# Windowed attention with a SoLU layer behind it: the one list that orders all five engines is laid out anew

## The chip, the cores and the metric

The kernel runs on one core of one Trainium2 chip. The metric is the device time of one launch in microseconds (us); lower is better. Its times before were 540.47 us in the median of three runs (538.63 to 542.15).

## The reference

Eight batches of eight heads with 576 positions and 64 channels go through attention with a window of 32. Heads 0 to 3 see the 32 latest positions, heads 4 to 7 every fourth of the 128 latest. The 4608 tokens of 512 values that come out go through a layer with two matrices, w_in (512 x 1024) and w_out (1024 x 512), both given in float64.

```python
scores = scale * np.matmul(q, k.transpose(0, 1, 3, 2))
scores = np.where(masks[None, :, :, :], scores, -1000000000.0)
attn = np.exp(scores - np.max(scores, axis=-1, keepdims=True))
attn = attn / (np.sum(attn, axis=-1, keepdims=True) + 1e-09)
x = np.matmul(attn, v)      # then heads side by side: (4608, 512)
h = x @ w_in
solu = h * softmax(h)
ln = (solu - mean(solu)) / np.sqrt(var(solu) + 1e-06) * g_ln
out = ln @ w_out
```

## The kernel before, in words

No scheduler decides anything here. `ORDER` (L61 to L125) is a list of 1200 words, such as `S10`, `V7` or `Ma3`: a name and a number. The kernel's last loop takes them one by one and calls the function that the table `do` has for the name; each engine gets its instructions in the order in which the words call for them. So the list sets the order on PE, DVE, ACT, POOL and in SP's queue of transfers at once. Semaphores are set where data or buffers demand it.

```python
for step in ORDER.split():
    name = step.rstrip("0123456789")
    do[name](int(step[len(name) :] or 0))
```

The words that the prediction speaks of:

- `c` loads constants, `q` and `v` load queries with keys, and values, of a unit (two heads of a batch; 32 units). `w` loads a group of weight blocks; `z` is a POOL memset that holds such a load back.
- `abs`, `low`, `hi`, `lo`, `gain` (ACT), `clamp`, `sign`, `join` (DVE) and `diff` (PE) turn the float64 weights of nine groups into a high and a low part. `ta` to `td`, `ua` to `ud`, `va` to `vd` make sums of blocks for the quick products.
- `S` n is the score word of a unit: 40 little products 32 x 64 in `scores` (L369, products at L382), which the trace shows as 80 instructions MATMUL (2560 over 32 units) and as many LDWEIGHTS. Units 0 to 5 have four more for the mask.
- `V` n is the value word, in `attend` (L466, L476): 48 or 40 little products, 96 or 80 MATMUL in the trace.
- Units go through the softmax in pairs u, as units 2u and 2u + 1: `pmask`, `pmax`, `psub`, `pexp`, `psum`, `pinv`, `pnorm`, `pturn` (DVE, but `pexp` on ACT, and `psub` and `pnorm` on POOL from pair 3 on). `pturn` (L458) is the transposition on DVE that the pair's two `V` wait for. `px` then copies the pair's results out of PSUM (ACT).
- The first matrix: for token tiles 0 to 3 the words `Ha` to `Hd` and `Ka` to `Kd`, of 3 products 128 x 512 each; from tile 4 on pairs p of tiles with the seven words `Ma` to `Mg` (a Strassen-like scheme), of 6 products each (L524). `hA`, `hB`, `hS`, `lA`, `lB`, `lS`, `s` make their operands; `ca` to `cg` take up the results.
- `peak`, `e`, `gate`, `mid`, `var`, `t`, `th`, `tl` are the SoLU and normalisation of a tile; `oa` to `od` its product with w_out, 6 products 128 x 512 each (L696); `out` stores it.

A product 128 x 512 is one LDWEIGHTS and one MATMUL. "Large products" below are those of `H`, `K`, `M`, `o` and `diff`; "small words" are `S` and `V`.

Of the kernel before, what the change touches and what calls it, by code (L numbers as in the profile page):

```python
# [58 lines left out]
LOWS = "t0 t1 e0 e1 w12 w13 x_sum w12".split()  # L59
H_BANK = {0: 2, 1: 0, 2: 2, 3: 0}  # L60
ORDER = (  # L61
# [63 lines left out]
)  # L125
PRODUCTS = {
    "Ma": (0, (0, 2), 0), "Mb": (8, (16, 17), 1), "Mc": (2, (4, 6), 0), "Md": (10, (21, 19), 1),
# [715 lines left out]
```

## Time and profile before

| | us |
|---|---|
| three runs: median (lowest to highest) | 540.47 (538.63 to 542.15) |
| the profiled execution: its time | 538.95 |
| its span, from the first to the last instruction | 536.4 |
| PE busy | 482.4 (90%) |
| DVE, ACT, POOL busy | 403.1 (75%), 315.9 (59%), 172.0 (32%) |

The span is what the rows of the trace add up to; 538.95 - 536.4 = 2.55 us lie around it. Times in the rows count from the span's start. A matmul's end is modelled, so that its successors seem to begin before it ends: a stream is timed from start to start. "Idle before" names what ended an engine's idle time; "issue" means that the engine waited for nothing that the profile shows.

### The profile page before, as it was taken

Reading aid. Unit: us, or ns where it says so; the run is one execution under the profiler, and the core shown is the slowest. Engines: PE = TensorE matmul, PEld = TensorE weight load, DVE = VectorE, ACT = ScalarE, POOL = GpSimd, SP = SyncE. Lnnn points to the kernel's source line nnn. Section 1 sums busy time; section 2 is a strip of 40 time slices with the busy share of each in tenths; the row PEclk is TensorE's granted clock in tenths of the full one; section 3 lists DMA queues with packets and bytes.
Section 4 is the critical chain, followed back from the end, with each engine's and each line's share of the span. In section 5 each row is a group of like instructions: output and inputs, shape, how many; then the busy total and the mean of one; then the engine's idle time right before and its main releaser. Section 6 shows DMA issues by size and latency. Waiting matters only on the chain.

```text
span 536.4 us, 16190 instructions
## 1 busy us (share of the span) xinstructions
PE 482.4 (90%) x7116; PEld 385.5 (72%) x7116; DVE 403.1 (75%) x632; ACT 315.9 (59%) x415; POOL 172.0 (32%) x262
## 2 busy tenths in 40 slices
PE   4648869899979799999998989998999899999997
PEld 2235658777858677788777767886887688888885
DVE  1887978898786598877778867797898967786341
ACT  3757778756545266664545655765483736466571
POOL 0202446632415053333423306242505243131121
PEclk9978979999979799999998989999999999999999
DMA  8991520321935423534441434443725141231011
GB/s 308 377 377 66 185 79 1 129 69 40 304 108 153 145 86 114 143 83 146 137 137 50 119 126 129 129 133 130 222 81 147 29 123 43 77 99 40 21 39 39
DMA packets 32693, 66.57 MB, mean 124 GB/s; under 512 B 3568, under 2 KB 18160, under 8 KB 32240
## 3 DMA queue, kind: packets, MB, share of 16 engines
q1 hardware_dynamic: 32480, 65.42, 38.2%
q8 instruction: 55, 0.90, 0.7%
q10 hardware_dynamic: 144, 0.13, 0.1%
q14 instruction: 14, 0.11, 0.1%
HBM read 41.42 MB, written 9.44 MB: 95 GB/s over the span
## 4 chain that ended last, share of the span: by engine, by line
PE 53%; DVE 23%; issue 8%; ACT 6%; POOL 5%; DMA 3%; SPq 1%; DVEq 0%; ACTq 0%; POOLq 0%
PE banks L696 24%; PE banks L524 18%; PE banks L476 6%; PE banks L382 3%; DVE t L614 3%; DVE x_lo L328 2%; POOL sm L455 2%; DVE pt L458 2%; DMA u<-b 2%; POOL sm L434 1%; DVE little L420 1%; DVE tl L328 1%; DVE little L445 1%; DVE sm L404 1%; DMA wt<-w_in 1%
## 5 line engine op out<-in xcount | busy, mean ns | idle before, releaser
L696 PE MATMUL banks<-wt,th 128*128 128x512 f32 x576 | 181.0, 398 | 1.3 <-ACT ob L713 1.2
L696 PEld LDWEIGHTS banks<-wt,th 128*128 128x128 f32 x576 | 107.7, 190 | 25.9 <-ACT ob L713 2.6
L696 PE MATMUL banks<-wt,tl 128*128 128x512 f32 x288 | 112.2, 393 | 0.0
L524 PE MATMUL banks<-wt,x_hi 128*128 128x512 f32 x320 | 103.2, 404 | 1.6 <-ACT wt L333 1.1
L524 PEld LDWEIGHTS banks<-wt,x_hi 128*128 128x128 f32 x320 | 60.7, 193 | 15.3 <-ACT wt L333 1.7
L524 PE MATMUL banks<-w,x_hi 128*128 128x512 f32 x192 | 63.2, 411 | 1.2 <-DVE t L578 1.2
L524 PE MATMUL banks<-wt,x_lo 128*128 128x512 f32 x160 | 63.9, 399 | 0.3 <-DVE x_lo L328 0.3
L434 POOL TENSOR_TENSOR sm<-sm,little 128x1280 f32<-128x1280 f32 x13 | 32.6, 2505 | 96.7 <-DVE little L420 78.0
L696 PEld LDWEIGHTS banks<-wt,tl 128*128 128x128 f32 x288 | 54.7, 190 | 11.7
L585 DVE CUSTOM_DVE_ANT_0 t<-banks,t 128x512 f32<-128x512 f32 x64 | 43.3, 685 | 24.1 <-PE banks L524 23.4
L608 ACT ACTIVATE e<-t,row 128x1024 f32<-128x1024 f32 x32 | 36.8, 1150 | 30.4 <-DVE row L591 30.4
L476 PE MATMUL banks<-pt,vt 32*64 32x64 f32 (+3 forms) x2816 | 35.9, 238 | 20.4 <-issue 15.2
L713 ACT ACTIVATE ob<-banks,row 128x512 f32<-128x512 f32 x35 | 24.0, 686 | 50.3 <-PE banks L696 36.2
L476 PEld LDWEIGHTS banks<-pt,vt 32*64 32x64 f32 x2816 | 33.6, 139 | 26.9 <-issue 18.1
L614 DVE CUSTOM_DVE_ANT_0 t<-t,e 128x1024 f32<-128x1024 f32 x32 | 40.5, 1269 | 9.6 <-ACT e L608 9.6
L382 PE MATMUL banks<-qk 64*32 64x64 f32 x2560 | 33.1, 235 | 14.9 <-issue 12.5
L669 ACT CAST th<-u 128x1024 fp32r<-128x1024 f32 x28 | 29.3, 1047 | 27.4 <-DMA u<-b 22.7
L382 PEld LDWEIGHTS banks<-qk 64*32 64x32 f32 x2560 | 28.4, 110 | 23.6 <-issue 17.5
L524 PEld LDWEIGHTS banks<-w,x_hi 128*128 128x128 f32 x192 | 36.6, 196 | 10.6 <-DVE t L578 2.2
L639 POOL TENSOR_SCALAR row<-row 128x1 f32<-128x1 f32 x36 | 8.8, 245 | 103.9 <-ACT e L634 102.8
L492 ACT COPY x_raw<-banks 128x1152 f32<-128x1152 f32 x16 | 26.9, 1682 | 23.3 <-PE banks L476 23.1
L635 POOL TENSOR_SCALAR row<-row 128x1 f32<-128x1 f32 x36 | 20.0, 555 | 64.3 <-ACT e L608 62.2
(107 smaller groups left out, 819.0 us busy)
## 6 DMA issues: line engine op xcount, KB each, us to landing
qk<-qk SPq DMA_DIRECT2D x32, 616.0 KB, 5.4
u<-b SPq DMA_DIRECT2D x112, 128.0 KB, 2.9
vt<-vw SPq DMA_DIRECT2D x32, 384.0 KB, 4.6
out<-ob SPq DMA_DIRECT2D x35, 256.0 KB, 2.4
wt<-w_out SPq DMA_DIRECT2D x4, 1024.0 KB, 10.8
wt<-w_in SPq DMA_DIRECT2D x3, 1024.0 KB, 14.3
wt<-w_in SPq DMA_DIRECT2D x2, 512.0 KB, 8.1
steady_sb<-steady SPq DMA_DIRECT2D x1, 260.0 KB, 4.1
```

The costliest lines, as they stand in the source:

```text
L382: nc.tensor.matmul(out=ps[WIN * c : WIN * c + WIN, h, WQ * i : WQ * i + WQ], lhsT=qt[D * h : D * h + D, q0 : q0 + WIN], rhs=kt[D * h : D * ...
L434: eng.tensor_tensor(out=rows(part(sm_sb, us)), in0=soft_source(us), in1=mx, op=ALU.subtract)
L476: nc.tensor.matmul(out=ps[D * h : D * h + D, c, c0 : c0 + k1 - k0], lhsT=vt[WIN * c : WIN * c + WIN, i, D * h : D * h + D], rhs=pt[WIN * c ...
L492: nc.scalar.copy(out=x.rearrange(form, c=NG), in_=ps[:, k : k + len(us), :, 0:GQ])
L524: nc.tensor.matmul(out=ps, lhsT=a[:, x], rhs=weights(w)[:, part, :], start=start and k == 0 and j == 0, stop=stop and k == last and j == 2 ...
L585: nc.vector.tensor_tensor_reduce(out=split_t(k)[half], in0=banks[:, c, :], in1=add, scale=1.0, scalar=-3.0e38, op0=ALU.add, op1=ALU.max, a ...
L608: nc.scalar.activation(out=e_sb[i % 2], in_=h_of(i), func=AF.Exp, bias=ms[i]["nmax"], scale=1.0, accum_out=se)
L614: nc.vector.tensor_tensor_reduce(out=t_sb[i % 2], in0=h_of(i), in1=e_sb[i % 2], scale=1.0, scalar=0.0, op0=ALU.mult, op1=ALU.add, accum_ou ...
L635: nc.gpsimd.tensor_scalar(out=se, in0=se, scalar1=1e-9, scalar2=None, op0=ALU.add)
L669: nc.scalar.copy(out=by_quarter(th), in_=u_sb[i % 2].rearrange("p g (k i) -> p k g i", k=FT))
L696: nc.tensor.matmul(out=ps_o(i), lhsT=a[:, f, :], rhs=weights(8 + f)[:, part, :], start=k == 0, stop=k == 3 * FT - 1,)
L713: nc.scalar.activation(out=ob, in_=ps_o(i), func=AF.Copy, scale=rstd)
```

## The change

Only `ORDER` is changed: the same 1200 words stand in another order, and no function differs. With them go all five engines and SP's queue. In the opening the loads go `c w0 w1 w2 q1 q0 w3 w4`, where they went `q0 c w1 q1 w0 w2 w3 w4`. Behind the opening the words `S` and `V` take other places. Before, the two `S` of each of the 16 pairs stand next to each other on PE, and the two `V` also. Now large products stand between the two `S` of five pairs (1, 2, 5, 6, 15) and between the two `V` of six (3, 6, 8, 12, 13, 15); the other pairs still stand together, at other places among the products. Between the later `S` of a pair and its first `V` there were at least 11 words of six large products in pairs 4 to 15; now there are 10 in pairs 5, 6, 7 and 14, 11 in pairs 4 (with the transpositions `t2` and `t3` besides), 13 and 15, and 13 or more in the others. The lines around pair 6 and pair 5:

```diff
-    "pnorm5 od2 pturn5 Mc3 hA4 tl5 Md3 V11 cd3 V10 Mf3 cc3 q14 ce3 cf3 out2 px5 Mg3 lA4 oa5 S13 "
-    "th4 v15 tl4 S12 hB4 e7 s4 ob5 gate7 hS4 cg3 mid7 oc5 q16 pmask6 pmax6 e6 od5 t7 out5 Ma4 "
...
+    "v13 e5 s3 v11 px4 cg2 ob3 lB3 S10 gate5 oc3 od3 hS3 e4 mid5 S11 out3 gate4 lS3 mid4 pmask5 "
+    "var5 pmax5 psub5 Ma3 t5 oa2 var4 Me3 ca3 Mb3 pexp5 Mc3 t4 ob2 cb3 Md3 psum5 th5 hA4 pinv5 oc2 "
+    "od2 out2 th4 q13 cd3 Mf3 cc3 pnorm5 pturn5 lA4 q12 V10 ce3 V11 Mg3 tl4 px5 Ma4 cf3 tl5 cg3 "
+    "oa5 s4 e6 gate6 hS4 S12 lS4 ob5 e7 gate7 oc5 s5 mid7 S13 pmask6 mid6 od5 pmax6 Mb4 psub6 out5 "
```

On PE, the score words of pair 6 (units 12 and 13) before; L382 with x40 is one `S`, an L696 row with `th` and x2 and one with `tl` are three large products:

```order
L696 MATMUL banks<-wt_723,th_1028 128x512 x2
L696 MATMUL banks<-wt_723,tl_1065 128x512
L696 MATMUL banks<-wt_723,th_1028 128x512 x2
L696 MATMUL banks<-wt_723,tl_1065 128x512
L382 MATMUL banks<-qk_83 32x64 x40
L382 MATMUL banks<-qk_82 32x64 x40
L696 MATMUL banks<-wt_706,th_1028 128x512 x2
L696 MATMUL banks<-wt_706,tl_1065 128x512
```

The same two words now:

```order
L382 MATMUL banks<-qk_82 32x64 x40
L696 MATMUL banks<-wt_737,th_1020 128x512 x2
L696 MATMUL banks<-wt_737,tl_1053 128x512
L696 MATMUL banks<-wt_737,th_1020 128x512 x2
L696 MATMUL banks<-wt_737,tl_1053 128x512
L696 MATMUL banks<-wt_684,th_1020 128x512 x2
L696 MATMUL banks<-wt_684,tl_1053 128x512
L696 MATMUL banks<-wt_684,th_1020 128x512 x2
L696 MATMUL banks<-wt_684,tl_1053 128x512
L382 MATMUL banks<-qk_83 32x64 x40
```

Twelve large products have come between the two score words.

On DVE, the softmax of pair 2 in the opening before (L420 is `pmax2`, L434 `psub2`, L604 `peak0`, L445 `psum2`, L614 `gate0`, L449 and L450 `pinv2`, L455 `pnorm2`, L458 `pturn2`):

```order
L420 TENSOR_REDUCE little<-banks 128x20
L434 TENSOR_TENSOR sm<-banks,little 128x1280
L604 TENSOR_REDUCE row<-banks 128x1
L445 TENSOR_REDUCE little<-sm 128x20
L614 ISA t_71,row<-banks,e_73 128x1024
L614 ISA row 128x1
L449 TENSOR_SCALAR little<-little 128x20
L450 RECIPROCAL little<-little 128x20
L624 TENSOR_SCALAR row<-row 128x1
L455 TENSOR_TENSOR sm<-sm,little 128x1280
L458 STREAM_TRANSPOSE pt<-sm 128x1280
```

The same stretch of DVE now:

```order
L420 TENSOR_REDUCE little<-banks 128x20
L434 TENSOR_TENSOR sm<-banks,little 128x1280
L445 TENSOR_REDUCE little<-sm 128x20
L449 TENSOR_SCALAR little<-little 128x20
L450 RECIPROCAL little<-little 128x20
L455 TENSOR_TENSOR sm<-sm,little 128x1280
L458 STREAM_TRANSPOSE pt<-sm 128x1280
L604 TENSOR_REDUCE row<-banks 128x1 x2
```

`peak0` and `gate0` (with its L624) have gone behind `pturn2`.

## Rows read from the trace of the kernel before

**Rows 1.** The page: busy time, share of the span, instructions; DMA queue, kind: packets, MB

```profile
PE 482.4 (90%) x7116; PEld 385.5 (72%) x7116; DVE 403.1 (75%) x632; ACT 315.9 (59%) x415; POOL 172.0 (32%) x262
...
q8 instruction: 55, 0.90, 0.7%
```

**Rows 2.** PE's waits from 93 us on: engine line <- awaited: total us, times, longest

```profile
PE banks L476 <- issue: 10.0, 4, 3.4
PE banks L382 <- issue: 7.5, 5, 2.5
...
PE banks L476 <- DVE pt L458: 0.8, 3, 0.4
```

**Rows 3.** PE's timeline, 149 to 162 us: start, length, what, count [idle before <- releaser]

```profile
150.50 1.48 PE L382 MATMUL banks<-qk 64*32 64x64 f32 x128 [0.62 <-issue]
154.50 0.45 PE L382 MATMUL banks<-qk 64*32 64x64 f32 x12 [2.52 <-issue]
154.88 1.22 PE L696 MATMUL banks<-wt,th 128*128 128x512 f32 x2
...
160.17 0.79 PE L696 MATMUL banks<-wt,th 128*128 128x512 f32 x2
...
161.03 0.62 PE L696 MATMUL banks<-wt,th 128*128 128x512 f32 x2
...
161.71 0.62 PE L524 MATMUL banks<-wt,x_hi 128*128 128x512 f32 x2
```

**Rows 4.** PE's timeline at other "issue" waits

```profile
34.47 0.42 PE L382 MATMUL banks<-qk 64*32 64x64 f32 x3 [3.89 <-issue]
34.82 2.16 PE L476 MATMUL banks<-pt,vt 32*64 32x32 f32 x125
41.04 1.25 PE L476 MATMUL banks<-pt,vt 32*64 32x64 f32 x67 [4.06 <-issue]
...
126.16 1.40 PE L382 MATMUL banks<-qk 64*32 64x64 f32 x119 [0.21 <-issue]
...
174.04 1.96 PE L476 MATMUL banks<-pt,vt 32*64 32x32 f32 x171
179.43 0.61 PE L476 MATMUL banks<-pt,vt 32*64 32x48 f32 x21 [3.42 <-issue]
```

**Rows 5.** Windows (three of the five): us, busy us (count) of PE, PEld, DVE, ACT, POOL, PEclk, DMA share, GB/s

```profile
153.68:160.51 6.83, 6.01 (x25) 4.68 (x26) 5.44 (x4) 1.73 (x3) 2.31 (x1) 0.50 0.30 96
177.57:184.40 6.83, 4.97 (x143) 3.90 (x145) 1.08 (x5) 2.07 (x2) 0.00 (x0) 0.50 0.20 60
...
426.75:430.16 3.41, 3.41 (x10) 2.64 (x9) 2.86 (x3) 1.72 (x3) 0.97 (x4) 0.50 0.62 134
```

**Rows 6.** DVE's timeline in the opening

```profile
46.16 1.51 DVE L458 STREAM_TRANSPOSE pt<-sm 128x1280 f32<-128x1280 f32 x1
47.59 1.18 DVE L303 SCALAR_TENSOR_TENSOR tl<-tl,x_sum 128x1024 int32<-128x1024 int32 x1
...
61.13 1.22 DVE L604 TENSOR_REDUCE row<-banks 128x1 f32<-128x1024 f32 x1
...
63.96 1.22 DVE L614 CUSTOM_DVE_ANT_0 t<-banks,e 128x1024 f32<-128x1024 f32 x1
...
69.65 1.51 DVE L458 STREAM_TRANSPOSE pt<-sm 128x1280 f32<-128x1280 f32 x1
```

**Rows 7.** PE's timeline: the value words of pairs 2 and 3

```profile
71.21 2.79 PE L476 MATMUL banks<-pt,vt 32*64 32x32 f32 x188 [4.31 <-DVE pt L458]
...
93.14 1.78 PE L476 MATMUL banks<-pt,vt 32*64 32x64 f32 x148
```

**Rows 8.** PE's timeline: end of the score words of pair 13

```profile
373.29 1.63 PE L382 MATMUL banks<-qk 64*32 64x64 f32 x136
```

**Rows 9.** DVE's timeline: the transpositions of pairs 6 and 13

```profile
171.17 1.51 DVE L458 STREAM_TRANSPOSE pt<-sm 128x1280 f32<-128x1280 f32 x1 [0.99 <-POOL sm L455]
...
387.40 1.51 DVE L458 STREAM_TRANSPOSE pt<-sm 128x1280 f32<-128x1280 f32 x1
```

120 rows, old and new, of the table ORDER are left out of this document.

## The prediction, written before the changed kernel ran

> **What bounds the kernel now.** I read the page first, to see which engine is full: PE, busy for 482.4 of 536.4 us, 90% [rows 1]. So the time is PE's work plus what PE loses, and I looked for the losses: in the list of waits, then in PE's timeline around the longest of them, then in windows for the granted clock.
>
> The list of waits gives the first loss. From 93 us on, when the opening is over, PE stands idle for 10.0 + 7.5 = 17.5 us in front of small products (L476, L382) with no releaser but "issue"; the wait for the softmax (DVE pt) is 0.8 us in all [rows 2]. The timeline shows where such a wait stands. The two S words of pair 6 are 160 MATMUL in a row. PE stops before 128 of them, runs those 128 in 1.48 us, stops for 2.52 us and does the last 12 [rows 3]. The same spacing stands in the opening: a stop, 3 + 125 = 128 MATMUL, a stop [rows 4]. 128 MATMUL with their 128 LDWEIGHTS are 256 instructions. The page's queue q8 moved 0.90 MB of instructions in 55 packets, and PE has 2 x 7116 instructions: 259 for each packet of 16.4 KB [rows 1]. I read this so: PE's program comes in blocks of 256 instructions, and the next block is usable only some time after the one before it was entered. With "line" for a block's beginning, that time can be read where PE had to wait: 154.50 - 150.50 = 4.0 us behind one line; in the opening, under the weight loads, 41.04 - 34.47 = 6.6 us [rows 3, 4]. A block of nothing but small products lasts 1.5 us, so it costs a stop of 2 to 3 us. A block with some large products lasts longer and costs little: the one that ends where the 119 MATMUL at 126.16 begin has six by my count (below), and the stop behind it is 0.21 us [rows 4].
>
> The second loss hangs on the first. In the windows the granted clock is 0.50, the lower of TensorE's two levels, from 153.68 to 160.51, from 177.57 to 184.40, and in three shorter windows of 3.4 us, each of which holds or follows such a stop [rows 5]. Twelve large products take 160.17 - 154.88 = 5.29 us there, and three take 161.71 - 161.03 = 0.68 us at the full level, which is 2.72 us for twelve [rows 3].
>
> **The change part by part.** It adds and removes nothing: the products are the same, at 0.68 / 3 = 0.227 us each. The sum goes against the profiled execution's span, 536.4 us.
>
> 1) The stops behind the opening, 17.5 us. I counted PE's list in steps of 256 instructions, a large product 2, an S word 160, a V word 192 or 160, from the line that row 34.47 fixes (three MATMUL before the end of the S words of pair 1), with some forty instructions that only wait counted too. In the list of before, behind pair 2's V words, eight blocks hold no large product at all: in the V words of pairs 3, 6, 10, 12 and 13 and the S words of pairs 6, 10 and 15; long stops stand at seven of them, all but pair 13's. In the new list no block there is without: one has 6 (V6, ob0 and V7), three have 9 or 10, all others 12 or more. Twelve large ones are 12 x 0.227 = 2.7 us, and with 116 small ones at 1.48 / 128 = 0.0116 us the block lasts 4.1 us, against the 4.0 us of row 150.50. The block with 6 lasts 1.4 + 1.4 = 2.8 us and may wait 0.2 (as at 126.16) to 1.2 us. Where a fetch takes as long as in the V words of pair 6, a block of twelve waits too: there 43 of the 171 MATMUL at 174.04 still belong to the block before (0.5 us), so it was 179.43 - 174.54 = 4.9 us [rows 4], 0.8 us more than the block lasts. I keep 2.5 us: -15.0, with ends -17.5 (all gone) and -10 (most blocks meet slow fetches).
>
> 2) The half clock. The five windows are 2 x 6.83 + 3 x 3.41 = 23.9 us. Of these PE waited 154.50 - 153.68 = 0.8 and 179.43 - 177.57 = 1.9 us, and some 2.5 us went to small words, whose pace falls little; half of the 18.7 us left is lost: -9.2. Without stops of 2 us I see nothing that would lower the level. Ends -9.2 and -5.
>
> 3) The opening. DVE sets it from 47 us on: pair 1's transposition ends at 47.67, pair 2's at 71.16, and PE idles 4.31 us until then [rows 6, 7]. Of the 23.5 us between, three operations go to the other side: join7 (1.18) ahead of the first transposition, peak0 and gate0 (1.22 each) behind the second [rows 6]; two shorter ones change sides and about cancel. That leaves 19.9 us. Ahead of pair 1's transposition, join7 is added, and the waits that PE's two stops of 3.89 and 4.06 us passed on to DVE [rows 4] are largely gone: S3 and S2 have diff3 between them, which gives the fetch its time. I put pair 1 at 44, so pair 2 at 64 and its V words 7 us earlier. From there to pair 3's V words it was 93.14 - 71.21 = 21.9 us [rows 7]; peak0 and gate0 come into this stretch (2.4 us at worst), while PE's loss in the first of these V words goes, so I keep 22: V6 at 86, but with six large products fewer before it (ob0 goes behind): 93.14 - 86 - 1.36 = 5.8 us gained. Against this stands the order of the loads: S0 now waits for three weight groups that go ahead of q0. Ends +1 and -10; I take -5.8.
>
> 4) New waits. Fewer stops, and S and V nearer to each other, give the softmax less room: what a pair needs from its last S to the end of pturn. Pair 13 shows 387.40 + 1.51 - 373.29 - 1.63 = 13.99 us, pair 6 shows 171.17 + 1.51 - 154.50 - 0.45 = 17.7 us [rows 3, 8, 9], both with PE not waiting or hardly. Between S and V pairs 5, 6, 7 and 14 now have ten words of six, 10 x 1.36 = 13.6 us; pairs 13 and 15 have 15.0. I take 14.5 us, near pair 13, since the new list puts pturn right ahead of V there, and pair 6 had 12 words and two stops to fill: 4 x 0.9 = +3.5, with ends 0 (13.6) and, at 15.6, 4 x 2.0 + 2 x 0.6 = +9. Queued behind a waiting V on PE are the large products of the next M and o, whose results DVE and ACT take up, so such a wait is not made good by other work.
>
> Sum: 536.4 - 15.0 - 9.2 - 5.8 + 3.5 = 509.9 us, and with the 2.55 us around the span 512.5. The profiled execution (538.95) was 1.5 us under the median, so 512.5 to 514; I forecast 513 us.
>
> [...]
>
> **The rivals.**
>
> a) The softmax takes over in part. DVE is at 75% [rows 1] and 27 us less time makes it 79%; each pair then needs 16 us from S to pturn. Four pairs wait 2.4 us and two 1.0, 11.6 us, and four waits over 2 us bring the half clock back at 9.2 / 5 = 1.8 us each: 18.8 us in place of 3.5, 528 us. For it: pair 6's 17.7 us. Against it: pair 13, and 0.8 us of such waits in all before.
>
> b) The stops stay. Either PE's program is there in time, and the idle time before small products is one that the order doesn't move; or my count of the lines is off by some tens of instructions, and S and V pairs that still stand together cover whole blocks again. Terms 1 and 2 fall away: 536.4 - 5.8 + 3.5 + 2.55 = 537 us, within 1% of before. [...] For the second: the new places hold by some tens of instructions only. Against both: stops 128 MATMUL apart, in two places [rows 3, 4], and a count that finds seven long stops of before.
>
> c) Slower: the chain S to pturn becomes the bound. If it needs 18.7 us, one more than pair 6 took, four pairs wait 5.1, two 3.7, pair 4 (16.9 us of room, two transpositions counted) 1.8, three with 13 words (17.7 us) 1.0 each: 32.6 us, with six half-clock windows 10.9 more. 43.5 - 15.0 - 9.2 - 5.8 = +13.5: 552 us. It decides from some 17.5 us on, where waits and clock eat the 30 us gained. Against it: POOL and DVE work on other things between a pair's steps when V isn't near, so 17.7 is no floor, and 14.0 was made.
>
> **How the numbers follow.** A difference of 1% is about what a measurement of this kernel can tell from none. My forecast, from 500 to 522 us, has a chance of 0.70; a) (522 to 534) 0.17; b) 0.08; c) 0.05. Faster: forecast and nearly all of a), 0.87; within 1% (535.1 to 545.9): b), 0.08; slower 0.05. The best ends of the terms give 536.4 - 17.5 - 9.2 - 10 + 2.55 = 502; the worst of the forecast 536.4 - 10 - 5 + 1 + 9 + 2.55 = 534, but not all at once. The range goes from 502 to 529, which takes in a) and leaves out b), c) and the tails.
>
> **What would show it.** Step 1: the "issue" waits of PE behind the opening fall from 17.5 us to under 5, and none is over 1.5 us. Step 2: granted clock 1.00 in all of the span from about 90 us on. Step 3: pair 2's V words begin near 64 us, pair 3's near 86. Step 4: waits for DVE pt at the V words of pairs 5, 6, 7 and 14, about 1 us each. Wrong would be: stops at other words with the same 128 MATMUL between them (b), or V words that wait 3 us and more with DVE's L458 as releaser (a, c).

## The result, and the profile after

| | before | after |
|---|---|---|
| runs beside each other: median (lowest to highest), us | 540.32 (538.63 to 542.15), 4 runs | 511.92 (510.17 to 514.58), 4 runs |
| ratio to before, 95% interval | | 0.948 (0.943 to 0.953) |
| the profiled execution: time, span | 538.95, 536.4 | 514.58, 512.8 |
| PE busy | 482.4 (90%) | 476.2 (93%) |

The changed list is 28.4 us faster in the median; 513 us had been forecast, in a range of 502 to 529. The two profiled executions are 24.4 us apart, because the one of before lay 1.4 us under its median and the one of after 2.7 us over its own. Their spans differ by 23.6 us, and these the trace accounts for. Ratios, here and below, leave out executions more than 1.5% above the fastest of their kernel, while medians take in all of them; of the kernel before, which spreads from 530.5 to 543.0 us over 19 executions, the ratios see the faster part alone.

The page of the kernel after, its busy times, PE's load in 40 slices and the granted clock, and the instruction queue (packets, MB, share):

```profile
PE 476.2 (93%) x7116; PEld 382.3 (75%) x7116; DVE 389.2 (76%) x632; ACT 315.4 (62%) x415; POOL 156.7 (31%) x262
...
PE   1958779999999998999999999998999999999997
...
PEclk9987779999999999999999999999999999999999
...
q8 instruction: 55, 0.90, 0.7%
```

The count of instructions and the 55 packets of program are those of [rows 1]; what has changed is that PE is nearly gapless from the seventh slice on, and that the clock there stays at its higher level: its two levels in the traces of before and after are 0.50 and 1.00, and from 78.4 to 511.8 us it is 1.00.

PE's waits in the kernel after, from 93 us on, as in [rows 2] (engine line <- awaited: total us, times, longest):

```profile
PE banks L382 <- issue: 3.3, 2, 1.8
PE banks L524 <- DVE t L578: 1.0, 1, 1.0
PE banks L382 <- ACT x_raw L492: 0.9, 1, 0.9
PE banks L382 <- DMA qk<-qk: 0.8, 1, 0.8
PE banks L476 <- issue: 0.6, 2, 0.4
...
PE banks L476 <- DMA vt<-vw: 0.2, 1, 0.2
```

The 17.5 us of "issue" have become 3.3 + 0.6 = 3.9 us, and the wait for the softmax (DVE pt) isn't in the list at all.

S8, the first score word of pair 4, begins at 99.93 us before and at 98.55 after, and both lists have the same PE work behind it. So the stretch from there to the end can be compared window by window (columns as in [rows 5]). Before:

```profile
99.90:536.40 436.50, 412.90 (x5593) 336.72 (x5592) 326.39 (x548) 247.82 (x332) 138.72 (x225) 0.97 0.37 110
```

After:

```profile
98.50:512.80 414.30, 404.11 (x5592) 330.23 (x5592) 315.33 (x544) 247.95 (x331) 128.04 (x228) 1.00 0.38 115
```

The same 5592 products take 412.90 - 404.11 = 8.8 us less, because the granted clock is 1.00 and no longer 0.97: that is the half-clock loss. PE's idle time falls from 436.50 - 412.90 = 23.6 to 10.2 us, 13.4 us less; 12.0 of it are "issue" stops (15.7 us from 100 us on before, 3.7 after), 1.4 other waits. Together 22.2 us; the other 1.4 us of the 23.6 by which the spans differ come from the opening, in this pair of executions.

PE's timeline of the kernel after: all the stops that are left (start, length, what, count [idle before <- releaser]):

```profile
39.35 1.25 PE L476 MATMUL banks<-pt,vt 32*64 32x64 f32 x68 [2.89 <-issue]
...
55.04 0.65 PE L382 MATMUL banks<-qk 64*32 64x64 f32 x23 [2.78 <-issue]
...
94.41 0.32 PE L476 MATMUL banks<-pt,vt 32*64 32x16 f32 x12 [0.18 <-issue]
...
172.50 0.66 PE L476 MATMUL banks<-pt,vt 32*64 32x64 f32 x39 [0.37 <-issue]
...
200.31 1.19 PE L382 MATMUL banks<-qk 64*32 64x64 f32 x99 [1.75 <-issue]
...
351.68 0.71 PE L382 MATMUL banks<-qk 64*32 64x64 f32 x47 [1.58 <-issue]
```

The one at 94.41 stands behind the block with six large products, where 0.2 to 1.2 us had been foreseen. The two long ones, at 200.31 and 351.68, stand behind blocks of 18 and 12 large products, and data were being loaded there. The window ahead of the first of them:

```profile
192.80:197.90 5.10, 5.10 (x107) 4.07 (x101) 3.53 (x10) 5.02 (x5) 0.00 (x0) 1.00 0.72 251
```

PE worked in all of the 5.10 us, with the 16 DMA engines at 0.72, and still had to wait 1.75 us for its next block. Neither of the two was followed by the half clock.

### The profile page after: what moved, and what is told of

Its sections match the earlier page's. It is cut to its first block, busy times and chain, and to the rows that moved or that the text cites. A ratio compares the mean times of both kernels' runs of the same rounds, so it can differ in the third digit from the quotient of the medians.

```text
span 512.8 us, 16184 instructions
## 1 busy us (share of the span) xinstructions
PE 476.2 (93%) x7116; PEld 382.3 (75%) x7116; DVE 389.2 (76%) x632; ACT 315.4 (62%) x415; POOL 156.7 (31%) x262
## 4 chain that ended last, share of the span: by engine, by line
PE 71%; DMA 11%; DVE 7%; ACT 4%; SPq 3%; issue 3%; POOL 0%; ACTq 0%; DVEq 0%; POOLq 0%
PE banks L696 32%; PE banks L524 28%; PE banks L476 5%; PE banks L382 4%; DMA vt<-vw 4%; DMA wt<-w_in 3%; DMA qk<-qk 2%; SPq L658 2%; DMA u<-b 2%; ACT x_raw L492 1%; DVE t L614 1%; PE banks L651 1%; DVE tl L328 1%; DVE row L604 1%; PE banks L324 1%
## 5 line engine op out<-in xcount | busy, mean ns | idle before, releaser
L696 PE MATMUL banks<-wt,th 128*128 128x512 f32 x576 | 179.4, 395 | 0.0
L696 PEld LDWEIGHTS banks<-wt,th 128*128 128x128 f32 x576 | 106.1, 188 | 22.9 <-ACT ob L713 0.8
L696 PE MATMUL banks<-wt,tl 128*128 128x512 f32 x288 | 111.1, 390 | 0.0
L524 PE MATMUL banks<-wt,x_hi 128*128 128x512 f32 x320 | 104.2, 408 | 2.3 <-DVE row L614 1.8
L524 PEld LDWEIGHTS banks<-wt,x_hi 128*128 128x128 f32 x320 | 60.4, 194 | 16.1 <-DVE row L614 1.9
L524 PE MATMUL banks<-wt,x_lo 128*128 128x512 f32 x160 | 63.9, 399 | 0.0
L434 POOL TENSOR_TENSOR sm<-sm,little 128x1280 f32<-128x1280 f32 x13 | 31.3, 2407 | 105.3 <-DVE little L420 91.2
L696 PEld LDWEIGHTS banks<-wt,tl 128*128 128x128 f32 x288 | 54.1, 188 | 11.6
L524 PE MATMUL banks<-w,x_hi 128*128 128x512 f32 x192 | 59.9, 393 | 1.0 <-DVE t L578 1.0
L585 DVE CUSTOM_DVE_ANT_0 t<-banks,t 128x512 f32<-128x512 f32 x64 | 43.0, 682 | 12.2 <-PE banks L524 11.6
L382 PE MATMUL banks<-qk 64*32 64x64 f32 x2560 | 32.9, 237 | 16.5 <-DMA qk<-qk 8.7
L382 PEld LDWEIGHTS banks<-qk 64*32 64x32 f32 x2560 | 28.5, 110 | 25.3 <-issue 11.7
L578 DVE TENSOR_TENSOR t<-banks,t 128x512 f32<-128x512 f32 x32 | 21.9, 685 | 28.9 <-PE banks L524 23.0
L629 ACT ACTIVATE t<-t,row 128x1024 f32<-128x1024 f32 x28 | 31.9, 1149 | 17.8 <-DVE row L624 17.8
L614 DVE CUSTOM_DVE_ANT_0 t<-t,e 128x1024 f32<-128x1024 f32 x32 | 39.5, 1243 | 3.7 <-ACT e L608 3.6
L524 PEld LDWEIGHTS banks<-w,x_hi 128*128 128x128 f32 x192 | 35.5, 188 | 8.9 <-DVE t L578 1.7
L328 DVE TENSOR_TENSOR tl<-u,th 128x1024 fp32r<-128x1024 f32 x28 | 34.0, 1219 | 7.9 <-ACT th L669 7.7
```

The source lines that it names most:

```text
L328: eng.tensor_tensor(out=out, in0=whole, in1=part.bitcast(F32), op=ALU.subtract)
L382: nc.tensor.matmul(out=ps[WIN * c : WIN * c + WIN, h, WQ * i : WQ * i + WQ], lhsT=qt[D * h : D * h + D, q0 : q0 + WIN], rhs=kt[D * h : D * ...
L434: eng.tensor_tensor(out=rows(part(sm_sb, us)), in0=soft_source(us), in1=mx, op=ALU.subtract)
L524: nc.tensor.matmul(out=ps, lhsT=a[:, x], rhs=weights(w)[:, part, :], start=start and k == 0 and j == 0, stop=stop and k == last and j == 2 ...
L585: nc.vector.tensor_tensor_reduce(out=split_t(k)[half], in0=banks[:, c, :], in1=add, scale=1.0, scalar=-3.0e38, op0=ALU.add, op1=ALU.max, a ...
L614: nc.vector.tensor_tensor_reduce(out=t_sb[i % 2], in0=h_of(i), in1=e_sb[i % 2], scale=1.0, scalar=0.0, op0=ALU.mult, op1=ALU.add, accum_ou ...
```

## The experiments

The theory: PE's program arrives in blocks of 256 instructions, a block of tiny products alone is over before the next is there, and the new list puts enough large products into every block. Its rival: the places of the blocks don't matter; the gain is that other words stand next to each other, so that PE waits less for the other engines. The two differ where the list stays and only the block lines move. Ratios are to runs of the kernel before on the same chip. The kernels are set against each other by their medians.

**Moving the lines without moving the work.** A word `pad64` of 64 products of 32 columns, 128 PE instructions whose result nothing reads, goes ahead of S8 into the changed list; a second kernel has 32 of them (half as many), a third 128, a whole block:

```diff
+    def pad(n):
+        for _ in range(n):
+            nc.tensor.matmul(
+                out=banks[0:32, 4, 420:452], lhsT=id_bf[:, 0:32], rhs=id_bf[:, 0:32],
+                start=True, stop=True, skip_group_check=True,
+            )
...
-    lA2 ub1 od0 S8 vb1 out0
+    lA2 ub1 od0 pad64 S8 vb1 out0
```

64 products, half a block:

> The changed list with one word more: 64 products 32 x 32 (bf16, 128 instructions, into a part of PSUM that nobody reads) right ahead of S8. Nothing else moves. Theory (lines every 256 instructions): the lines behind that point fall 128 instructions earlier among the words, and the count finds eight blocks with no or one large product again where the changed list had none. Eight stops of 1.5 to 3 us come back, 13 to 18 us, with half-clock windows 5 to 10 us more, and about 1 us for the 64 products: 532 to 540 us. Rival (what counts is which words stand beside S and V, and what the other engines do meanwhile): only the 64 products are paid, 512.5 to 514 us.

128 products, a whole block:

> The changed list with 128 such products (256 instructions) right ahead of S8. Theory: the lines fall by a whole block, so among the words behind they stand where the changed kernel has them, and one block of nothing but these products is added: 1.5 to 2 us for them, one stop of about 2 us, perhaps one half-clock window of 2 us, 515 to 518 us, and less than with half as many products. Rival: twice the price of the 64 products, more than with 64.

32 products, a quarter of a block:

> The changed list with 32 of the little products (64 instructions) right ahead of S8; they take about 25 ns each, as in the run with 128, so 0.8 us. Theory: behind that point the count finds four blocks with no or one large product and one with four, where the changed list has none and the list with 64 products eight. Stops of 6 to 10 us come back, with one to three half-clock windows 2 to 5 us: 519 to 526 us, between the changed kernel and the one with 64 products. Rival: 0.8 us more than the changed kernel, 513 us.

| changed list with | median, us | ratio to before | PE "issue" from 100 us on | S8 to the end |
|---|---|---|---|---|
| nothing | 511.92 | 0.948 (0.943 to 0.953) | 3.7 | 414.3 |
| 32 products | 527.27 | 0.976 (0.969 to 0.983) | 12.1 | 429.4 |
| 64 products | 528.06 (10 runs) | 0.987 (0.981 to 0.993) | 14.2 | 431.5 |
| 128 products | 518.37 | 0.974 (0.969 to 0.979) | 3.3 | 414.8 |

The last two columns are of the profiled executions; that of the 64 products took 531.73 us, 3.7 over its median. Its waits of PE, from 100 us on (columns as above):

```profile
PE banks L476 <- issue: 6.3, 3, 3.4
PE banks L382 <- issue: 4.1, 4, 1.8
PE banks L524 <- issue: 3.8, 4, 1.7
PE banks L476 <- DMA vt<-vw: 1.2, 1, 1.2
PE banks L382 <- DMA qk<-qk: 1.1, 1, 1.1
```

The stops are back, though no word of the list has another neighbour, and no wait for DVE or ACT of note has come with them. They even stand before large products (L524), where the waits of neither list show one behind S8. Two of them in PE's timeline, and the window behind the second:

```profile
362.11 1.34 PE L382 MATMUL banks<-qk 64*32 64x64 f32 x111 [1.82 <-issue]
...
410.53 0.32 PE L476 MATMUL banks<-pt,vt 32*64 32x16 f32 x12 [3.44 <-issue]
```

```profile
411.20:414.60 3.40, 3.40 (x10) 2.62 (x9) 1.12 (x4) 1.51 (x3) 0.00 (x0) 0.50 0.02 5
```

Windows of this kind, at a granted clock of 0.50, stand behind four of its stops. The whole block of pads, with twice the products, is 9.7 us faster than the half: the lines are where they were, and little more than the pads is paid for (518.37 - 511.92 = 6.4 us, of which 3.3 are the pads and 1.4 a stop behind them). The rival, by which all three would cost no more than their own length, falls. Two of the three ranges were missed a little: 518.37 lies 0.4 us above its own (515 to 518), 528.06 lies 4 us under its own (532 to 540). In the list with half a block, seven blocks behind S8 hold no large product and one holds two; with a quarter, four hold none or one; in the changed list none does. The price doesn't follow that count (16.1 and 15.4 us): the quarter had been put at 519 to 526 and is beyond it. One reason is in the trace: three of the seven blocks, with lines at 143.50, 264.81 and 389.56 us, cost no stop. Their lines stand at most 16 small products behind large ones, and the packet with the next block (these packets are looked at below, at the nine S8) begins 1.0 to 2.0 us before such a line, at 141.50, 263.62 and 388.56. The changed list's layout is good for the one phase that it was counted for.

**One half of the list at a time.** Up to S8 the one list and from S8 on the other (the few words that would be missing or double are brought ahead of S8 or left out behind it).

The list of before up to S8, the changed one behind:

> The list of before up to S8, the remaining words in the changed order. Theory: the stops behind 93 us (17.5 us before) fall to about 4 and the half clock there (9 us) is gone; the opening is as before, V6 at about 93 us: 511 to 515 us, as the opening of the changed kernel gained only 1 us. Rival (the gain comes from the opening and from what it does to the rest): over 525 us.

The changed list up to S8, the one of before behind:

> The changed list up to S8, the remaining words in the order of before. Theory: stops behind 93 us as before, all seven long ones at the same words, and the half clock after them: 535 to 540 us. Rival (the opening carries the gain): under 525 us.

| | median, us | ratio | "issue" from 100 us on | S8 begins | S8 to the end |
|---|---|---|---|---|---|
| before | 538.66 (19 runs) | | 15.7 | 99.9 | 436.5 |
| new remainder | 516.7 | 0.971 (0.965 to 0.978) | 1.0 | 102.1 | 415.1 |
| new opening | 534.0 (10 runs) | 1.001 (0.997 to 1.005) | 16.2 | 98.4 | 438.3 |
| after | 511.92 | 0.948 (0.943 to 0.953) | 3.7 | 98.5 | 414.3 |

(First row: time of these 19 runs, columns of the profile before.) The remainder is worth 538.66 - 516.7 = 22.0 us, the opening 538.66 - 534.0 = 4.7 us, and in the other order 511.92 beside 534.0 and 516.7 gives 22.1 and 4.8. By its ratio of 1.001 the new opening alone is worth nothing, so that its share is not settled between none and some 5 us; the remainder's is clear by either. How early S8 begins speaks for a gain: 99.9, 102.1 and 104.3 us in three executions with the old opening, 97.3 to 98.6 us in five with the new (where pads stand ahead of S8, the first of them begins at 96.6, 96.8 and 99.5). The medians lie beside the expected ranges: 516.7 is 1.7 us above 511 to 515, 534.0 is 1 us under 535 to 540. With the old remainder the old stops stand at the old words, as in [rows 3, 4]:

```profile
151.93 1.49 PE L382 MATMUL banks<-qk 64*32 64x64 f32 x128 [0.97 <-issue]
...
155.94 0.33 PE L382 MATMUL banks<-qk 64*32 64x64 f32 x12 [2.52 <-issue]
...
179.84 0.41 PE L476 MATMUL banks<-pt,vt 32*64 32x48 f32 x21 [3.50 <-issue]
```

**One word of the list of before.** S12 goes behind oc5, so that twelve large products (ob5 and oc5) come between the score words of pair 6, whose stop of 2.52 us stands in [rows 3].

```diff
-    th4 v15 tl4 S12 hB4 e7 s4
+    th4 v15 tl4 hB4 e7 s4
...
-    cg3 mid7 oc5 q16 pmask6
+    cg3 mid7 oc5 S12 q16 pmask6
```

> The kernel before with one word moved: S12 stands behind oc5, twelve large products behind S13, where it stood next to it. Theory: the block between 150.50 and 154.50 us then holds twelve large products, its stop of 2.52 us goes and with it the half-clock window from 153.68 to 160.51 (2.6 us): 4 to 6 us less than before, if pair 6's softmax, with 10 words left to its V instead of 12, makes it in 14 us; all other stops stay. Rival (the stops belong to score and value words wherever they stand): the stop moves along, no difference.

538.02 us in the median of 10 runs (540.06 before), ratio 0.994 (0.988 to 1.000): too little to be told by the time alone. In the trace the stop and its half clock are gone, and from S10 to V14 it is 75.1 us, where it was 78.5. The expected 4 to 6 us came out as 3.4, and the rows of pair 6's value words show why:

```profile
174.28 1.97 PE L476 MATMUL banks<-pt,vt 32*64 32x32 f32 x171 [0.85 <-DVE pt L458]
180.36 0.62 PE L476 MATMUL banks<-pt,vt 32*64 32x48 f32 x21 [4.11 <-issue]
```

PE comes to V13 before the transposition is done (0.85 us), and at the next line, which hasn't moved, it stops for 4.11 us in place of 3.42 [rows 4]: the block came no sooner for PE being ahead. One stop less gave its length less what was late next.

**The price of a block by itself.** S8 stands nine times in the changed list: 8 x 160 = 1280 instructions more, five blocks of tiny products and nothing else.

```diff
-    od0 S8 vb1 out0
+    od0 S8 S8 S8 S8 S8 S8 S8 S8 S8 vb1 out0
```

> The changed list with S8 nine times in a row (the same products into the same place, 8 x 160 = 1280 instructions more, five whole blocks). It measures the disputed cost by itself: how fast PE gets through small products when its program has to be fetched for them alone. Theory: stops with 128 MATMUL between them, 3.4 to 4 us from stop to stop, five of them: 16 to 20 us more than the changed kernel (528 to 532 us), the stops behind as in the changed kernel. Rival (small products in a row are only bound by their issue): 8 x 1.0 us = 8 us more, 520 us.

One run: 536.11 us, 24 us more than the changed list, for 16 to 20 expected. PE's timeline:

```profile
98.27 2.49 PE L382 MATMUL banks<-qk 64*32 64x64 f32 x232 [1.45 <-ACT x_raw L492]
103.20 1.49 PE L382 MATMUL banks<-qk 64*32 64x64 f32 x128 [2.44 <-issue]
109.67 2.06 PE L382 MATMUL banks<-qk 64*32 64x64 f32 x128 [4.99 <-issue]
113.13 2.06 PE L382 MATMUL banks<-qk 64*32 64x64 f32 x128 [1.40 <-issue]
116.86 2.05 PE L382 MATMUL banks<-qk 64*32 64x64 f32 x128 [1.67 <-issue]
120.58 1.12 PE L382 MATMUL banks<-qk 64*32 64x64 f32 x56 [1.68 <-issue]
```

and its windows, from the second of these rows to the third and from the third to the last:

```profile
103.20:109.67 6.47, 1.49 (x128) 1.32 (x128) 0.00 (x0) 0.09 (x1) 0.00 (x0) 0.72 0.68 224
109.67:120.58 10.91, 6.16 (x384) 5.44 (x384) 0.00 (x0) 0.00 (x0) 0.00 (x0) 0.50 0.02 5
```

The stops are 128 MATMUL and 128 LDWEIGHTS apart, four times in a row, at words that wait for no other engine. With the DMA engines nearly still (0.02), from line to line it takes 113.13 - 109.67 = 3.46 us, then 3.73 and 3.72; with them at 0.68 it took 6.47. The 232 that ran without a stop are the last 104 of one block and the 128 of the next: one block was there in advance here, not several. The five stops make 12.2 us, and the 640 MATMUL at full clock 7.4; the rest of the 24 us fits the half clock, which lasts to 126.5 us and at which 128 of these products take 2.06 and not 1.49 us.

The blocks can be seen to arrive: the trace times each packet of q8, the queue of the instructions. Behind the line at 103.20 the DMA engines move data alone until 107.20, and in the 0.1 us after that the packet begins (windows 103.20 to 107.20, then 107.20 to 107.30; queue, kind: packets, MB, share of the 16 engines):

```profile
q1 hardware_dynamic: 353, 1.23, 94.9%
...
q1 hardware_dynamic: 15, 0.03, 78.4%
q8 instruction: 1, 0.02, 62.2%
```

Behind the line at 109.67, with nothing else to move, the packet begins at 110.82 (window 110.80 to 110.90):

```profile
q8 instruction: 1, 0.02, 61.8%
```

The five stops end 2.3 to 2.7 us after the beginning of a packet (at 100.85, 107.22, 110.82, 114.17 and 117.92). The same holds in all twelve traces: from 93 us on they have 65 stops of over 0.15 us that end without a releaser, and each ends 2.2 to 3.3 us after a packet's beginning. At each, too, PE's MATMULs and LDWEIGHTS so far, divided by 256, give in whole blocks the number of packets begun. So the "issue" of these stops is PE waiting for its program. What made a fetch late was the time before its packet began. Behind the lines that a stop marks it is 1.0 to 1.7 us with the DMA engines at less than 0.15, with one exception (3.0 us); in 13 cases it is 2.4 us or more, and in all of these but that one the engines were at 0.74 to 1.02 meanwhile. Two lines of the kernel before lie between, with 1.88 us at 0.55 (283.14 us) and 1.96 us at 0.99 (310.42 us).

**The changed list once more, and two attempts to better it.** The first kernel is the changed list itself; the second has S5 behind Ka0, to give the fetch ahead of the stop at 55.04 more time; the third brings four loads to places away from the two stops that were left (q17 up behind S13, as shown, q18 down behind S17, q29 and v29 down behind S26).

```diff
-    sign6 clamp6 yd0 S5 v5 Ha0 hi7 Ka0 v4
+    sign6 clamp6 yd0 v5 Ha0 hi7 Ka0 S5 v4
```

```diff
-    oc6 cb5 od6 q17 th9 q18 out6
+    oc6 cb5 od6 th9 out6
...
-    s5 mid7 S13 pmask6
+    s5 mid7 S13 q17 pmask6
```

> The changed list once more, on the chip of the three runs beside it. 509 to 515 us, as its first four runs (510.2 to 514.6).

> The changed list with S5 moved behind Ka0, so that nine large products instead of three stand between S4 and S5. Theory: the opening's gain was small because PE stops there too: the stop of 2.78 us at 55.04 falls under 1 us, V4 comes 1.5 to 2.5 us earlier than at 67.4, the whole 1 to 3 us under the changed kernel. Rival (DVE bounds the opening): V4 stays at 67 to 68, no difference.

> The changed list with four loads moved: q17 up behind S13, q18 behind S17, q29 and v29 behind S26. PE's order is the same. Theory (a block's fetch comes late while loads fill the DMA engines): the stops of 1.75 us at 200.31 and 1.58 us at 351.68 go, both of which stand behind blocks with 18 and 12 large products in which the DMA share was 0.72 and 0.88: 2 to 4 us under the changed kernel. Rival (those two are something else): they stay at the same words.

Medians of 511.97 (ratio 0.952, 0.943 to 0.960), 512.37 (0.951, 0.945 to 0.957) and 512.7 us (0.953, 0.946 to 0.960): no difference. With S5 moved PE still stops, and the window ahead of the stop shows a thing that the place of the word doesn't change:

```profile
56.68 0.45 PE L382 MATMUL banks<-qk 64*32 64x64 f32 x29 [2.45 <-issue]
```

```profile
50.00:53.50 3.50, 3.50 (x95) 2.56 (x94) 1.49 (x3) 3.50 (x6) 0.01 (x1) 1.00 0.98 379
```

The DMA engines are full (0.98) while the block is due; its packet begins at 54.24. With the loads moved, the stop near 352 us stayed (1.86 us), since SP issued the loads ahead of it when it had before (qk, vt and qk from 343.27 to 345.04 us, against 342.65 to 344.08 in the kernel after). The stop at 200.31 is gone there: SP issues one load of qk ahead of that block (at 192.30 us) where it issued two in the kernel after (from 190.37), and the packet begins 1.8 us behind the line and no longer 5.1. The same block in the other traces of this list fits: 4.3 us and a stop of 0.88 in the plain repetition, 3.4 us and no stop with S5 moved. So late fetches went with data being moved, in these four and in the windows shown here (DMA share 0.72, 0.68 and 0.98); each is one execution, and no run took the traffic away and nothing else. No kernel here beats the changed one.

## Why the prediction was right

**The reading of the bound** holds. Blocks of 256 instructions, and a new block some 4 us after the last line, or later under load: the nine S8 words show both (3.46 to 3.73, and 6.47 us), the pads show that the places of the lines decide and not the neighbours, and the packets of the instruction queue stand ahead of every stop. Why pair 13's block of before cost no stop, which the prediction left open, is to be seen there too: the packet with the next block begins at 388.57 us, 1.5 us before the line at 390.07, which stands six small products behind large ones. The nine S8 also show why a block of products of 12 ns alone is over too soon: its 128 MATMUL with their loads are through in 1.5 us, and the next block came 3.46 to 6.47 us after it was entered. Rival b) falls in both its forms: the program was not there in time, and the count of the lines was right. That a shift by some tens of instructions would undo the gain was right too, by 15 us for 64.

**Term 1, the stops behind the opening:** -15.0 forecast, 3.9 - 17.5 = -13.6 measured. The allowance of 2.5 us for late fetches was 1.4 short, and two stops are over the 1.5 us that the forecast set as the longest: it took the fetch of 4.9 us for the slow case, and at 192.80 the packet alone began 5.1 us behind the line. The count had left out one short block, the one right behind pair 2's V words (from 71.79 us, with about five large products by the trace); it cost no stop.

**Term 2, the half clock:** -9.2 forecast (half of 18.7 is 9.35, a slip of 0.15), -8.8 by PE's busy time for the same 5592 products. The forecast let the pace of the small words fall little; at 0.50 it fell more than that (128 products took 2.06 us in the nine S8, and 1.49 at full clock). In the kernel after the clock is 1.00 from 78.4 to 511.8 us. Not every stop brought the lower level: the two of 1.75 and 1.58 us in the kernel after were followed by none, while one of 1.71 us with S5 moved was (0.50 from 349.0 to 352.4 us).

**Term 3, the opening:** -5.8 forecast, measured to V6: by the same reckoning it is 93.14 - 90.73 - 1.36 = 1.05 us in the two profiled executions, and up to S8 between nothing (ratio) and 4.7 us (medians) in the half lists. This is the term that was furthest off. DVE's part came nearly as worked out. Pairs 1 and 2 in DVE's timeline after, beside [rows 6]:

```profile
41.83 1.51 DVE L458 STREAM_TRANSPOSE pt<-sm 128x1280 f32<-128x1280 f32 x1
...
63.67 1.51 DVE L458 STREAM_TRANSPOSE pt<-sm 128x1280 f32<-128x1280 f32 x1
```

They end at 43.3 and 65.2 us, for 44 and 64 forecast; the stretch between them took 21.8 us, 2 more than the 19.9 of the forecast. But PE doesn't follow:

```profile
67.35 2.19 PE L476 MATMUL banks<-pt,vt 32*64 32x32 f32 x192
71.34 1.07 PE L524 MATMUL banks<-wt,x_hi 128*128 128x512 f32 x2 [1.80 <-DVE row L614]
...
90.73 1.08 PE L476 MATMUL banks<-pt,vt 32*64 32x64 f32 x80
```

V4 begins at 67.35 without a wait: by then PE itself is late, from its stop at 55.04 and the half clock behind it (0.50 from 54.5 to 61.3 us). Behind V5 it waits 1.80 us for gate0 (L614), one of the two operations that went behind the transposition (2.4 us at worst, in the forecast), and the clock is at 0.50 again until 78.4; in the repetition of the same list the wait was the same and the clock stayed up. V6 came at 90.73 and not at 86. The step that failed is the one that let PE be ready whenever DVE was: it counted the two stops of before as gone, and they came back as 2.89 and 2.78 us, at other words. Their packets begin at 37.01 and 52.40 us, behind loads that fill the DMA engines (0.96 from 31.32 us, where the line before it is, and 0.98 from 49.42); the block ahead of the second holds only three large products.

**Term 4, new waits at the value words:** +3.5 forecast, none measured. The latency from a pair's last score word to the end of its transposition was taken as 14.5 us; pairs 5, 6, 7 and 14 needed 12.8, 13.8, 12.9 and 13.2. Pair 5, with its score word, transposition and value word:

```profile
126.27 1.04 PE L382 MATMUL banks<-qk 64*32 64x64 f32 x80
```

```profile
138.64 1.51 DVE L458 STREAM_TRANSPOSE pt<-sm 128x1280 f32<-128x1280 f32 x1 [0.25 <-POOL sm L455]
```

```profile
141.06 1.19 PE L476 MATMUL banks<-pt,vt 32*64 32x64 f32 x89
```

138.64 + 1.51 - 126.27 - 1.04 = 12.8 us, and PE comes 0.9 us later. Pair 6 of before (17.7 us) had more room and took it: a latency read where nobody waited was no floor, and even pair 13's 13.99 us [rows 8, 9] was above it. Rivals a) and c) rest on longer ones and fall with this.

So the sum was good partly by balance. Of the 23.6 us between the profiled spans 13.6 are the stops, 8.8 the half clock, 1.4 other waits of PE behind S8, which had no term, and the rest is the opening, -0.2 us once its last stop (1.8 us before, 0.2 after, between V6 and S8) is left to term 1. Forecast were 26.5: 1.4 too much in term 1, 0.4 in term 2, 6.0 in term 3; against that 3.5 for waits that didn't come and the 1.4 of the others. In the medians of the half lists the opening gained more, 4.7 - 1.6 = 3.1 us, but its size is not settled.

Open is why 19 executions of the kernel before spread over 12 us, and eight of the changed one over 7 (509.96 to 517.28): stops that depend on when data are moved would do that, but this is not shown.

## What to carry to other kernels

When an engine's idle time has no releaser and ends at an even distance in instructions, count its program in blocks of that size and give each block enough long instructions to outlast the fetch; here a dozen of 0.23 us sufficed where little data was being moved, and 18 did not where the packet had to wait 5.1 us. If the trace times the packets of the instruction queue, look for one ahead of each stop: that tells a fetch from idle time of another cause. Such a layout holds for one phase: after any edit ahead of it count again (64 instructions cost 15.4 us here). And take a latency for a new, tighter place from the pair that had the least room, as an upper end (here pair 13's 13.99 us, where 12.8 to 13.8 were needed).

## What the runs showed of the hardware that was not expected

- A pad product (32 columns, bf16) takes 26 ns from start to start, where a score product of 64 takes 11.6 ns. So a whole block of pads (3.3 us) lasts nearly as long as the 3.46 to 3.73 us from line to line in the nine S8, and PE stopped only in the S8 behind it, for 1.42 us:

```profile
99.46 3.35 PE L728 MATMUL banks<-steady_sb 128*32 128x32 bf16 x128 [0.85 <-ACT x_raw L492]
...
105.44 0.78 PE L382 MATMUL banks<-qk 64*32 64x64 f32 x56 [1.42 <-issue]
```

- The fetch didn't wait for PE's clock: with the DMA engines at 0.02 or less the packet begins 1.04 to 1.15 us behind the lines at 109.67, 113.13 and 116.86 of the nine S8, at a granted clock of 0.50, and 1.13 and 1.05 us behind those at 200.31 and 351.68 of the kernel after, at 1.00.
- While large products ran, the program was fetched ahead of what PE was executing: in the kernel after the packet with the next block begins at 183.33 us, 4.5 us before PE reaches the line at 187.87.
- A load's place in the list was not its time. q29 and v29 were put further back in the list, and SP issued the loads there from 343.27 to 345.04 us, after 342.65 to 344.08 in the kernel after.
